# A hand-woven order for VectorE, ScalarE and TensorE up to the last pair, with one factor block, the late turns and the filter tables moved, in an attention and FFT-gate kernel

## The chip, the cores and the metric

The kernel runs on one core of a Trainium2 chip. The metric is the device time of one execution in microseconds (us), here the median of the runs shown. A profiled execution has a time of its own, and a span from its first to its last instruction; both are named where they are used.

## What is computed

Batch 4, 8 heads, 768 positions, head size 64. Some heads (`is_retrieval`) attend to all earlier positions, the others to 4 sink positions and a window of 64. The attention's output, heads side by side, goes into a gate with a circular convolution along the sequence:

```python
scores = np.where(mask, scale * np.matmul(q, k.transpose(0, 1, 3, 2)), -1e9)
a = softmax(scores)                                 # scale = 1/8
x = np.matmul(a, v)                                 # B, H, S, D -> B, S, 512
x1, x2, x3 = split(x @ w_proj)                      # 512 channels each
x2_conv = irfft(rfft(x2) * rfft(filter_fft))        # along the 768 positions
out = (x1 * x2_conv * x3) @ w_out
```

(shortened from the reference). Inputs and output are float32.

## The kernel before

The work is cut into 16 pairs n = 0 to 15: batch b = n // 4 and head pair hp = n % 4. A pair is the attention of two heads; four pairs fill the transposed input xT of one batch's gate.

**A pair.** Loads of q, k and v go out on SP (SyncE) up to three pairs ahead (`emit_loads` L89, `emit_load_v` L97); POOL (GpSimd) casts them to bf16 (`emit_cast` L116, `emit_v` L302). `emit_prep` (L126) turns q and k so that the head dimension lies on the partitions: for n < 6 by TensorE (PE) and a copy on ScalarE (ACT, L140), from 6 on by a transposing DMA on SP (L142). The transposed scores of the causal blocks are computed in six chunks, two in each third (`emit_chunks` L311, matmul L322), each followed by an exp on ACT from PSUM into pT (L329). A mask product on VectorE (DVE) per third (`emit_masking` L331, L336) zeroes what isn't attended. A pair later come the products with v and a column of ones (`emit_values` L339, 42 matmuls, L347), the division (`emit_norm` L354: `rec` L357, `attn` L358, both DVE) and the turn of attn into xT (`emit_turn` L361: six PE transposes L365 and a DVE copy L367 for n < 6 and for the last pair of each batch; a transposing DMA on SP, L369, for the others).

**A gate.** `moe(b, xT)` (L374) is a generator; each `gate_step` (L480) runs it to its next `yield`. Its steps before the change, with the PE work of each:

- x2, three steps: eight 512-column matmuls (L380), a copy on ACT (L384), a sum and a difference on DVE (L385, L386);
- X, three steps: six 512-column matmuls with the Fourier matrix G (`emit_forward` L253, L258), a copy on ACT (L392), products with the filter tables on DVE into P (L395 to L401);
- factors, four blocks of two steps (L404 to L421): eight 384-column matmuls each (L411); the first half is copied by ACT (x1s, L418), the second is multiplied into g by DVE (L420);
- c, four steps: eight 384-column matmuls with the inverse matrix Gi (L427), ACT copy evs (L430), DVE conv and y (L432 to L434);
- out, three steps: eight 512-column matmuls (L439), ACT copy (L448), DMA of the output on SP (L449). The gate of the last batch writes six blocks (L453 to L466).

**Filter tables.** `setup_steps` (L266) folds the filter (DVE, L269, L270) and makes the tables HAB in four more steps: an `emit_forward` each, with copies and edits on ACT and DVE (L275 to L298).

**The order of the work.** The loop over n (from L501) issues scores, masks, values and gate steps in a fixed text order. SP and POOL always run in that order (`manual_schedule`, L105). PE, ACT and DVE run in it only while n < `MANUAL` = 5 (L103, `order.close()` L507); from then on a scheduler arranges their instructions when the program is built, taking the text order as priority. All matmul results share one pool of four PSUM buffers of two banks each (`bank_pair`, L79 to L82), given out in turn.

The Fourier matrix G has tiles 4 to 7, which hold the halves of G2 twice; before the change four DMAs on SP fill them in pair 1 (L517 to L521). The DMA transpose of G to Gi is issued on SP in pair 5 (L572).

Of the kernel before, what the change touches and what calls it, by code (L numbers as in the profile page):

```python
# [10 lines left out]
BF16 = mybir.dt.bfloat16  # L11
# [33 lines left out]
def kernel(  # L45
# [13 lines left out]
    nc = tc.nc  # L59
# [3 lines left out]
    DM = moe_w_proj.shape[0]  # L63
# [20 lines left out]
    state = {}  # L84
# [15 lines left out]
        nc.sync.dma_start(out=vf, in_=v[b, 2 * hp:2 * hp + 2].rearrange("h (t p) d -> p h t d", p=128))  # L100

    BY_PE = 6
    MANUAL = 5  # L103
    engine = mybir.EngineType
    ctx.enter_context(tc.manual_schedule(engines={engine.Pool, engine.SP}))  # L105
    order = ExitStack()
# [135 lines left out]
    def emit_matrix():  # L242

        nc.gpsimd.tensor_scalar(out=G[:, 1, :, 0], in0=par.to_broadcast([128, NM]), scalar1=-2.0, scalar2=1.0,
                                op0=ALU.mult, op1=ALU.add)

    Gi = const.tile([128, 8, NM, 128], BF16, name="Gi")

    def emit_inverse_matrix():
# [121 lines left out]
                in_=st["attn"].rearrange("p t hh d -> p (t hh d)"))  # L371


    def moe(b, xT):  # L374
        x2 = msb.tile([128, 2, NM, DM], BF16, name="x2")
        for m in range(NM):
            ps = bank_pair("x2_ps")
            for half in range(2):
                for cc in range(NC):
                    nc.tensor.matmul(ps[:, half, :], lhsT=xT[:, cc, half * HS + m * 128:half * HS + (m + 1) * 128],  # L380
                                     rhs=wproj[:, cc, DM:2 * DM],
                                     start=(cc == 0), stop=(cc == NC - 1))
            x2s = msb2.tile([128, 2, DM], BF16, name="x2s")
            nc.scalar.copy(out=x2s, in_=ps)  # L384
            nc.vector.tensor_add(x2[:, 0, m, :], x2s[:, 0], x2s[:, 1])  # L385
            nc.vector.tensor_sub(x2[:, 1, m, :], x2s[:, 0], x2s[:, 1])  # L386
            yield
        P = msb.tile([128, 4, 2, DM], BF16, name="P")
        for t in range(3):
            X = msb2.tile([128, 2, DM], BF16, name="X")  # L390
            ps = emit_forward(x2, ((0, 0), (1, 1)), G2) if t == 2 else emit_forward(x2, ((2 * t, t), (2 * t + 1, t)))
            nc.scalar.copy(out=X, in_=ps)  # L392
            yield
            if t == 2:
                nc.vector.tensor_mul(P[:, 2:4], X[:, None].to_broadcast([128, 2, 2, DM]),  # L395
                                     HAB[:, 2].rearrange("p (a r) c -> p a r c", a=2))
                continue
            nc.vector.tensor_mul(P[:, t], X, HA[:, t])  # L398
            m2 = msb2.tile([128, 2, DM], BF16, name="m2")
            nc.vector.tensor_mul(m2, X[:, ::-1, :], HB[:, t])  # L400
            nc.vector.tensor_add(P[:, t], P[:, t], m2)  # L401
        g = msb.tile([128, NC, S], BF16, name="g")
        y = msb.tile([128, NC, S], BF16, name="y")
        for cb in range(NC):  # L404
            ch = slice(cb * 128, (cb + 1) * 128)
            halves = []
            for part in (0, 2):
                ps = bank_pair("x13_ps")
                for s in range(2):
                    for cc in range(NC):  # L410
                        nc.tensor.matmul(ps[:, s, 0:HS],  # L411
                                         lhsT=wproj[:, cc, part * DM + cb * 128:part * DM + (cb + 1) * 128],
                                         rhs=xT[:, cc, s * HS:s * HS + HS],
                                         start=(cc == 0), stop=(cc == NC - 1))
                halves.append(ps[:, :, 0:HS])
                if part == 0:
                    x1s = msb2.tile([128, 2, HS], BF16, name="x1s")
                    nc.scalar.copy(out=x1s, in_=halves[0])  # L418
                    yield
            nc.vector.tensor_mul(g[:, cb, :].rearrange("p (s t) -> p s t", s=2), x1s, halves[1])  # L420
            yield  # L421
        for cb in range(NC):
            ch = slice(cb * 128, (cb + 1) * 128)
            ps = bank_pair("c_ps")
            for r in range(2):
                for n, (tile_no, t, u) in enumerate(((2 * r, r, 0), (2 * r + 1, r, 1), (4 + r, 2, r), (6 + r, 3, r))):
                    nc.tensor.matmul(ps[:, r, 0:HS], lhsT=P[:, t, u, ch], rhs=Gi[:, tile_no],  # L427
                                     start=(n == 0), stop=(n == 3))
            evs = msb2.tile([128, HS], FP32, name="evs")
            nc.scalar.copy(out=evs, in_=ps[:, 0, 0:HS])  # L430
            conv = msb2.tile([128, S], BF16, name="conv")
            nc.vector.tensor_add(conv[:, 0:HS], evs, ps[:, 1, 0:HS])  # L432
            nc.vector.tensor_sub(conv[:, HS:S], evs, ps[:, 1, 0:HS])  # L433
            nc.vector.tensor_mul(y[:, cb, :], conv, g[:, cb, :])  # L434
            yield
        def emit_out(ps, i, cbs):
            for cb in cbs:
                for n in range(ps.shape[1]):
                    nc.tensor.matmul(ps[:, n, :], lhsT=y[:, cb, (i + n) * 128:(i + n + 1) * 128],  # L439
                                     rhs=wout[:, cb, :], start=(cb == 0), stop=(cb == NC - 1))  # L440

        if b < B - 1:
            for i in range(0, NT, 2):
                ps = bank_pair("out_ps")
                for n in range(2):
                    emit_out(ps[:, n:n + 1], i + n, range(NC))
                o_sb = msb2.tile([128, 2, DM], FP32, name="o_sb")
                nc.scalar.copy(out=o_sb, in_=ps)  # L448
                nc.sync.dma_start(  # L449
                    out=out[b, i * 128:(i + 2) * 128, :].rearrange("(n p) c -> p n c", p=128), in_=o_sb)  # L450
                yield
            return
        o_last = pTp.tile([128, NT, DM], FP32, name="o_last", tag="pT")  # L453
        ps = [bank_pair("out_ps")[:, 0:1] for i in range(3)]
        for cbs in ((0, 1), (2,), (3,)):
            for i in range(3):
                emit_out(ps[i], i, cbs)
        for i in range(NT):
            if i >= 3:
                ps.append(bank_pair("out_ps")[:, 0:1])  # L460
                emit_out(ps[i], i, range(NC))
            if i % 2:
                nc.vector.tensor_copy(out=o_last[:, i], in_=ps[i][:, 0])
            else:
                nc.scalar.copy(out=o_last[:, i], in_=ps[i][:, 0])
            nc.sync.dma_start(out=out[b, i * 128:(i + 1) * 128, :], in_=o_last[:, i])  # L466
        yield
# [20 lines left out]
    def emit_weights(n):  # L488
        if n == 0:
            state["filt"] = filt = msb.tile([128, NT, DM], BF16, name="filt", tag="g")  # L490
            nc.gpsimd.dma_start(out=filt, in_=moe_filter_fft.rearrange("(t p) c -> p t c", p=128))
            emit_matrix()
        for part in {2: (1,), 4: (0, 2)}.get(n, ()):
            cols = slice(part * DM, part * DM + DM)
            nc.gpsimd.dma_start(out=wproj[:, :, cols], in_=moe_w_proj.rearrange("(c p) n -> p c n", p=128)[:, :, cols])
        if n == 7:
            nc.gpsimd.dma_start(out=wout, in_=moe_w_out.rearrange("(c p) n -> p c n", p=128))
# [3 lines left out]
    for n, (b, hp) in enumerate(pairs):  # L501
# [12 lines left out]
            emit_v(state[n + 1])  # L514
        if 1 <= n < N - 3:
            emit_loads(n + 3)
        if n == 1:  # L517
            for part in range(2):
                for half in range(2):
                    nc.sync.dma_start(out=G[:, 4 + 2 * part:6 + 2 * part, :, 64 * half:64 * half + 64],  # L520
                                      in_=G2[:, :, :, 64 * part:64 * part + 64])  # L521
        if n < 4:
            if n >= 2:
                emit_turn(state[n - 2])
# [14 lines left out]
                emit_norm(last)  # L539
            emit_chunks(st, 2, 1)  # L540
            emit_masking(st, 1)
            if n == 3:
                gates.append(setup_steps())
                gate_step()
            continue
        if n == 4:
            emit_turn(state[n - 2])
            emit_masking(last, 2)
        elif n + 1 < BY_PE:
            emit_prep(nxt)  # L550
        gate_step()
        emit_values(last)
        emit_norm(last)
        emit_masking(st, 0)
        if n > 4:
            gate_step()
        emit_chunks(st, 1)
        if n == 4:
            gate_step()
        emit_masking(st, 1)  # L560
        emit_turn(last)
        if n == 4:
            emit_prep(nxt)
        if BY_PE <= n + 2 < N:
            emit_prep(state[n + 2])
        gate_step()
        if hp == 0:
            gates.append(moe(b - 1, last["xT"]))
        gate_step()
        emit_chunks(st, 2)  # L570
        emit_masking(st, 2)
        if n == 5:  # L572
            emit_inverse_matrix()
        gate_step()
    last = state[N - 1]
    emit_values(last)
    emit_norm(last)
# [41 lines left out]
```

## Time and profile before

| | us |
|---|---|
| median of 3 runs (lowest to highest) | 225.52 (224.45 to 227.03) |
| profiled execution: its time | 226.71 |
| its span | 225.0 |
| PE busy | 192.8 |
| DVE busy | 160.5 |
| ACT busy | 150.3 |
| POOL busy | 70.6 |
| first scores of pair 4 / 5 / 9 / 13 | 33.06 / 50.28 / 99.27 / 144.67 |
| last attention product (pair 15) | 178.10 |

In a table of stretches each engine has its busy time and, in brackets, its instructions; PEld is PE's loading of weights, PEclk the granted clock of PE as a share of full speed, DMA the mean busy share of the 16 DMA engines. In the list of waits the numbers are: us in total, how often, longest. In a timeline they are: start, duration, then engine, line and operation, and in square brackets the idle time before and what ended it. PE's matmuls overlap, so their pace is read from starts that follow each other.

### The profile page before, as it was taken

Reading aid. Unit: us, or ns where it says so; the run is one execution under the profiler, and the core shown is the slowest. Engines: PE = TensorE matmul, PEld = TensorE weight load, DVE = VectorE, ACT = ScalarE, POOL = GpSimd, SP = SyncE. Lnnn points to the kernel's source line nnn. Section 1 sums busy time; section 2 is a strip of 40 time slices with the busy share of each in tenths; the row PEclk is TensorE's granted clock in tenths of the full one; section 3 lists DMA queues with packets and bytes.
Section 4 is the critical chain, followed back from the end, with each engine's and each line's share of the span. In section 5 each row is a group of like instructions: output and inputs, shape, how many; then the busy total and the mean of one; then the engine's idle time right before and its main releaser. Section 6 shows DMA issues by size and latency. Waiting matters only on the chain.

```text
span 225.0 us, 4244 instructions
## 1 busy us (share of the span) xinstructions
PE 192.8 (86%) x1726; PEld 103.0 (46%) x1726; DVE 160.5 (71%) x251; ACT 150.3 (67%) x183; POOL 70.6 (31%) x99
## 2 busy tenths in 40 slices
PE   1579876779878999799987999899899989999991
PEld 0335554335344645335353654353556644455630
DVE  6979889996896769815697679547876682466681
ACT  7999996657874776187984684779885423662321
POOL 5399447906430643600346062412000000000000
PEclk9999999999999999799999999999999999999999
DMA  5999999999999999648996999298011001500007
GB/s 153 301 297 211 274 188 262 187 222 213 199 184 215 203 183 224 63 186 196 176 221 122 218 180 188 68 309 109 0 38 35 3 1 66 214 3 0 0 3 277
DMA packets 93027, 34.81 MB, mean 155 GB/s; under 512 B 84048, under 2 KB 89936, under 8 KB 93008
## 3 DMA queue, kind: packets, MB, share of 16 engines
q1 hardware_dynamic: 90112, 31.67, 69.5%
q0 software_dynamic: 2896, 2.88, 7.9%
q8 instruction: 13, 0.21, 0.4%
q14 instruction: 6, 0.05, 0.1%
HBM read 24.65 MB, written 6.29 MB: 138 GB/s over the span
## 4 chain that ended last, share of the span: by engine, by line
PE 46%; DVE 29%; ACT 17%; issue 3%; DMA 2%; POOL 0%; SPq 0%; ACTq 0%; DVEq 0%
PE x_ps L411 17%; ACT pT L329 10%; PE out_ps L439 9%; PE x_ps L380 6%; DVE pT L336 5%; PE sc L322 4%; PE att L347 3%; PE c_ps L427 3%; PE X_ps L258 3%; DVE attn L358 3%; DVE y L434 2%; ACT qkT L140 2%; DVE conv L432 2%; DVE P L401 2%; DVE P L398 2%
## 5 line engine op out<-in xcount | busy, mean ns | idle before, releaser
L329 ACT ACTIVATE pT<-sc 128x1024 bf16<-128x1024 f32 x96 | 83.0, 966 | 9.5 <-PE sc L322 9.4
L336 DVE TENSOR_TENSOR pT<-pT,mask 128x1024 bf16<-128x1024 bf16 x48 | 41.8, 873 | 20.9 <-ACT pT L329 20.4
L114 POOL CAST qk_bf<-qk_f 128x768 bf16<-128x768 f32 x31 | 27.1, 878 | 71.8 <-DMA qk_f<-in_q_dram 60.4
L411 PE MATMUL x_ps<-xT,wproj 128*128 128x384 bf16 x256 | 45.3, 326 | 3.4 <-DVE attn L358 1.9
L322 PE MATMUL sc<-qkT 64*128 64x512 bf16 (+3 forms) x256 | 29.9, 326 | 6.5 <-ACT qkT L140 2.5
L411 PEld LDWEIGHTS <-wproj 128*128 128x128 bf16 x256 | 23.8, 98 | 21.1 <-issue 5.6
L347 PE MATMUL att<-v_aug,pT 128*128 128x65 bf16 x352 | 25.3, 197 | 3.1 <-DVE pT L336 2.6
L347 PEld LDWEIGHTS <-pT 128*128 128x128 bf16 x672 | 23.8, 100 | 8.2 <-DVE pT L336 4.1
L420 DVE TENSOR_TENSOR g<-x1s,x_ps 128x768 bf16<-128x768 bf16 x16 | 15.2, 952 | 14.4 <-PE x_ps L411 14.3
L439 PE MATMUL out_ps<-wout,y 128*128 128x512 bf16 x96 | 24.3, 401 | 1.1 <-DVE conv L433 0.6
L380 PE MATMUL x_ps<-wproj,xT 128*128 128x512 bf16 x96 | 22.4, 379 | 1.2 <-DVE HAB L277 1.0
L427 PE MATMUL c_ps<-Gi,P 128*128 128x384 bf16 x128 | 22.8, 326 | 0.0
L418 ACT CAST x1s<-x_ps 128x768 bf16<-128x768 f32 x16 | 12.8, 801 | 14.4 <-PE x_ps L411 14.4
L347 PE MATMUL att<-v_far,pT 128*128 128x65 bf16 x320 | 21.9, 197 | 0.0
L322 PEld LDWEIGHTS <-qkT 64*128 64x128 bf16 x256 | 9.6, 96 | 26.1 <-issue 18.4
L309 POOL TENSOR_TENSOR v_far<-v_aug,vmask 128x520 bf16<-128x520 bf16 x16 | 20.0, 1249 | 1.3
L430 ACT COPY evs<-c_ps 128x384 f32<-128x384 f32 x16 | 7.7, 482 | 15.7 <-PE c_ps L427 10.8
L114 POOL CAST v_aug<-v_f 128x768 bf16<-128x768 f32 x16 | 16.8, 1052 | 3.4 <-DMA v_f<-in_v_dram 3.4
L258 PE MATMUL X_ps<-x,G 128*128 128x512 bf16 x72 | 17.4, 379 | 0.3 <-ACT x2s L384 0.3
L384 ACT CAST x2s<-x_ps 128x1024 bf16<-128x1024 f32 x12 | 12.2, 1018 | 7.5 <-PE x_ps L380 5.3
L448 ACT COPY o_sb<-out_ps 128x1024 f32<-128x1024 f32 x9 | 9.1, 1012 | 10.0 <-PE out_ps L439 9.8
L358 DVE TENSOR_TENSOR attn<-att,rec 128x768 bf16<-128x768 f32 x16 | 15.3, 953 | 0.4
(76 smaller groups left out, 206.6 us busy)
## 6 DMA issues: line engine op xcount, KB each, us to landing
qk_f<-in_q_dram SPq DMA_DIRECT2D x16, 384.0 KB, 6.2
qk_f<-in_k_dram SPq DMA_DIRECT2D x16, 384.0 KB, 6.8
v_f<-in_v_dram SPq DMA_DIRECT2D x16, 384.0 KB, 5.0
out_dram<-o_sb SPq DMA_DIRECT2D x9, 512.0 KB, 3.1
wproj<-in_moe_w_proj_dram POOLq DMA_DIRECT2D x3, 512.0 KB, 7.7
out_dram<-o_last SPq DMA_DIRECT2D x6, 256.0 KB, 2.6
filt<-in_moe_filter_fft_dram POOLq DMA_DIRECT2D x1, 768.0 KB, 9.9
wout<-in_moe_w_out_dram POOLq DMA_DIRECT2D x1, 512.0 KB, 8.7
```

The source lines that it names most:

```text
L114: nc.gpsimd.tensor_copy(out=out, in_=in_)
L258: nc.tensor.matmul(ps[:, u, :], lhsT=matrix[:, t, m, :], rhs=src[:, r, m, :], start=(m == 0), stop=(m == NM - 1))
L309: nc.gpsimd.tensor_mul(v_far, v_aug[:, 0:4], vmask[:, hp, :, :, None].to_broadcast([128, 4, 2, 65]))
L322: nc.tensor.matmul(sc[:, hh, n * 128:(n + cnt) * 128], lhsT=qkT[rows, 1, j * 128:(j + 1) * 128], rhs=qkT[rows, 0, i * 128:(i + cnt) * 128] ...
L329: nc.scalar.activation(out=pT[:, :, c, 0:w], in_=sc[:, :, 0:w], func=AF.Exp, scale=SCALE)
L336: nc.vector.tensor_mul(near, near, kinds)
L347: nc.tensor.matmul(att[:, hh, 65 * i:65 * i + 65], lhsT=st["pT"][:, hh, c, 128 * n:128 * n + 128], rhs=st["v_far" if i >= j + 2 else "v_au ...
L358: nc.vector.tensor_mul(st["attn"].rearrange("p i hh d -> p hh i d"), rows[:, :, :, 0:64], rec[:, :, :, None].to_broadcast([128, 2, NT, 64]))
L380: nc.tensor.matmul(ps[:, half, :], lhsT=xT[:, cc, half * HS + m * 128:half * HS + (m + 1) * 128], rhs=wproj[:, cc, DM:2 * DM], start=(cc = ...
L411: nc.tensor.matmul(ps[:, s, 0:HS], lhsT=wproj[:, cc, part * DM + cb * 128:part * DM + (cb + 1) * 128], rhs=xT[:, cc, s * HS:s * HS + HS], ...
L427: nc.tensor.matmul(ps[:, r, 0:HS], lhsT=P[:, t, u, ch], rhs=Gi[:, tile_no], start=(n == 0), stop=(n == 3))
L439: nc.tensor.matmul(ps[:, n, :], lhsT=y[:, cb, (i + n) * 128:(i + n + 1) * 128], rhs=wout[:, cb, :], start=(cb == 0), stop=(cb == NC - 1))
```

## The change

- `MANUAL` goes from 5 to 15: PE, ACT and DVE run in the order of the text for pairs 0 to 14; the scheduler arranges pair 15 and what follows.
- The doubled tiles of G are written by four POOL copies in pair 3 (`emit_doubles`) in place of four DMAs on SP in pair 1.
- In the gate, the first factor block comes ahead of the X steps, the other three after them.
- The filter tables are made in pairs 4 and 5 (fold, then three steps in pair 4, the fourth in pair 5), the last two woven between the first x2 steps of gate 0 (`between`). Before, the fold was in pair 3 and the four steps in pair 4.
- In pairs 5 to 15 the turn of the pair before comes at the end of the pair, after the q/k transposes and the output DMAs of the middle; only in the first pair of a batch it stays before the start of the new gate. The gate steps are placed anew: five per pair, six in the odd ones.
- x2 and the folded filter have the same memory in both kernels. With the new order the first x2 sums are written there ahead of the last two table steps, which changes those two tables.

```diff
-    MANUAL = 5
+    MANUAL = 15
...
+    def emit_doubles():
+        for part in range(2):
+            for half in range(2):
+                nc.gpsimd.tensor_copy(out=G[:, 4 + 2 * part:6 + 2 * part, :, 64 * half:64 * half + 64],
+                                      in_=G2[:, :, :, 64 * part:64 * part + 64])
...
-    def moe(b, xT):
+    def moe(b, xT, between=()):
...
             yield
+            for step in between:
+                yield
+                break
         g = msb.tile([128, NC, S], BF16, name="g")
         y = msb.tile([128, NC, S], BF16, name="y")
-        for cb in range(NC):
-            ch = slice(cb * 128, (cb + 1) * 128)
+
+        def factors(cb):
             halves = []
...
+        yield from factors(0)
+        P = msb.tile([128, 4, 2, DM], BF16, name="P")
+        for t in range(3):
...
+        for cb in range(1, NC):
+            yield from factors(cb)
...
+        if n == 3:
+            emit_doubles()
...
-        if n == 1:
-            for part in range(2):
-                for half in range(2):
-                    nc.sync.dma_start(out=G[:, 4 + 2 * part:6 + 2 * part, :, 64 * half:64 * half + 64],
-                                      in_=G2[:, :, :, 64 * part:64 * part + 64])
...
-            if n == 3:
-                gates.append(setup_steps())
-                gate_step()
             continue
         if n == 4:
             emit_turn(state[n - 2])
             emit_masking(last, 2)
-        elif n + 1 < BY_PE:
+            setup = setup_steps()
+            next(setup)
+            emit_values(last)
+            emit_norm(last)
+            emit_chunks(st, 1)
+            next(setup)
+            emit_masking(st, 0)
+            emit_turn(last)
+            next(setup)
+            emit_masking(st, 1)
+            emit_prep(nxt)
+            gates.append(moe(b - 1, last["xT"], setup))
+            gate_step()
+            gate_step()
+            emit_prep(state[n + 2])
+            emit_chunks(st, 2)
+            emit_masking(st, 2)
+            gate_step()
+            continue
+        if n + 1 < BY_PE:
             emit_prep(nxt)
         gate_step()
         emit_values(last)
         emit_norm(last)
+        gate_step()
         emit_masking(st, 0)
-        if n > 4:
-            gate_step()
         emit_chunks(st, 1)
-        if n == 4:
-            gate_step()
+        gate_step()
         emit_masking(st, 1)
-        emit_turn(last)
-        if n == 4:
-            emit_prep(nxt)
+        if hp == 0:
+            emit_turn(last)
+            gates.append(moe(b - 1, last["xT"]))
         if BY_PE <= n + 2 < N:
             emit_prep(state[n + 2])
-        gate_step()
-        if hp == 0:
-            gates.append(moe(b - 1, last["xT"]))
         gate_step()
         emit_chunks(st, 2)
         emit_masking(st, 2)
         if n == 5:
             emit_inverse_matrix()
+        if hp != 0:
+            emit_turn(last)
         gate_step()
+        if hp % 2:
+            gate_step()
```

More of the change, by code (lines that the diff above doesn't have):

```diff
@@ L387, in moe @@
             yield
[L388 to L401, printed above, removed]
+            for step in between:
+                yield
+                break
         g = msb.tile([128, NC, S], BF16, name="g")
         y = msb.tile([128, NC, S], BF16, name="y")
-        for cb in range(NC):
-            ch = slice(cb * 128, (cb + 1) * 128)
+        def factors(cb):
             halves = []
@@ L421, in moe @@
             yield
+        yield from factors(0)
+        P = msb.tile([128, 4, 2, DM], BF16, name="P")
+        for t in range(3):
+            X = msb2.tile([128, 2, DM], BF16, name="X")
+            ps = emit_forward(x2, ((0, 0), (1, 1)), G2) if t == 2 else emit_forward(x2, ((2 * t, t), (2 * t + 1, t)))
+            nc.scalar.copy(out=X, in_=ps)
+            yield
+            if t == 2:
+                nc.vector.tensor_mul(P[:, 2:4], X[:, None].to_broadcast([128, 2, 2, DM]),
+                                     HAB[:, 2].rearrange("p (a r) c -> p a r c", a=2))
+                continue
+            nc.vector.tensor_mul(P[:, t], X, HA[:, t])
+            m2 = msb2.tile([128, 2, DM], BF16, name="m2")
+            nc.vector.tensor_mul(m2, X[:, ::-1, :], HB[:, t])
+            nc.vector.tensor_add(P[:, t], P[:, t], m2)
+        for cb in range(1, NC):
+            yield from factors(cb)
         for cb in range(NC):
@@ L548 @@
             emit_masking(last, 2)
-        elif n + 1 < BY_PE:
+            setup = setup_steps()
[16 more added lines that the diff above has]
+            gate_step()
+            continue
+        if n + 1 < BY_PE:
             emit_prep(nxt)
```

## The prediction

> **What bounds the kernel now.** First the share of busy time on the page, then the same by stage.
>
> ```profile
> PE 192.8 (86%) x1726; PEld 103.0 (46%) x1726; DVE 160.5 (71%) x251; ACT 150.3 (67%) x183; POOL 70.6 (31%) x99
> ```
>
> TensorE (PE) has most work, but no engine is full. In the timeline of PE I took the start of each pair's first scores (pair 5 at 50.28, 9 at 99.27, 12 at 132.39, 15 at 166.76) and of the last attention product (178.10), and asked for the busy time between these marks.
>
> ```profile
> core 0: us, PE busy (x) PEld busy (x) DVE busy (x) ACT busy (x) POOL busy (x), PEclk, DMA share, GB/s
> ...
> 74.69:84.25 9.56, 9.56 (x99) 5.48 (x98) 6.66 (x10) 6.91 (x10) 5.77 (x8) 1.00 1.15 201
> 84.25:99.27 15.02, 13.13 (x105) 6.31 (x105) 10.28 (x16) 8.08 (x12) 5.46 (x7) 0.89 0.81 141
> ...
> 110.77:122.84 12.07, 9.77 (x98) 5.36 (x98) 10.37 (x12) 8.09 (x11) 6.99 (x9) 1.00 0.91 165
> 122.84:132.39 9.55, 9.55 (x99) 5.50 (x100) 6.04 (x8) 6.88 (x9) 2.40 (x5) 1.00 1.08 194
> 132.39:144.67 12.28, 11.15 (x106) 5.77 (x106) 10.84 (x19) 7.88 (x12) 5.54 (x7) 1.00 0.99 145
> ...
> sum 127.82, PE 117.74 PEld 61.83 DVE 89.88 ACT 90.91 POOL 39.09; mean PE 10.70 PEld 5.62 DVE 8.17 ACT 8.26 POOL 3.55
> ```
>
> One line is one pair. Pairs 7 and 11 hold the attention of a pair and five gate steps of eight 384-column matmuls: PE never stops, 9.56 and 9.55 us. Where it stops, VectorE (DVE) is at 10 us of 12. Over pairs 5 to 15 PE is idle for 127.8 - 117.7 = 10.1 us. Before that, from 33 to 50 (pair 4 and the filter tables), PE has 11.94 busy of 17.00 and DVE 16.75: DVE is the bound there. After 178.1 there is one gate alone: 41.35 of 47. The waits of PE in 50 to 178 say who ends its pauses:
>
> ```profile
> PE xt_ps L365 <- DVE attn L358: 3.5, 4, 1.8
> PE x_ps L411 <- DVE attn L358: 1.9, 1, 1.9
> PE att L347 <- DVE pT L336: 1.5, 1, 1.5
> ```
>
> The second is what in-order queues do: the attention's PSUM buffer is freed by `attn` (L358), which stands on DVE behind the products P of L398 to L401, and PE needs that buffer. In the timeline of DVE the same product takes 0.69 or 1.3:
>
> ```profile
> 111.06 0.69 DVE L398 TENSOR_TENSOR P<-X,HAB 128x1024 bf16<-128x1024 bf16 x1 [0.47 <-ACT X L392]
> 111.67 1.31 DVE L400 TENSOR_TENSOR m<-X,HAB 128x1024 bf16<-128x1024 bf16 x1
> 112.90 1.30 DVE L398 TENSOR_TENSOR P<-X,HAB 128x1024 bf16<-128x1024 bf16 x1
> ...
> 118.62 0.94 DVE L358 TENSOR_TENSOR attn<-att,rec 128x768 bf16<-128x768 f32 x1
> ```
>
> **What the Trainium skill says.** "SBUF — State Buffer", section Who interferes with whom: a VectorE instruction with two SBUF inputs shares a read interface with GpSimd, and the second to start waits. The doubled durations agree: GpSimd (POOL) is busy 6.99 us in that pair, and from 155 on, with POOL silent, the same products are at 0.69. "Perfetto Trace Analysis", section Identifying the Most-Contended Engine, warns that matmul busy time says little of PE's headroom. It holds here, so I count steps, not shares. [...] The trace has one such stretch, granted clock 0.66 in 92 to 97, right after PE idled for 1.8 us.
>
> **The change part by part.**
>
> *Table copies from SP to POOL.* Four transfers go (6.93 us of SP's issue from 20.09) and four copies of 384 bf16 elements each come on POOL in pair 3. No row shows that copy; a 768-element cast (0.88) and the 520-element product (1.25) bound one at 0.4 to 1.25 us, 1.8 to 5 together; I take 2. POOL waits 4.26 us for q just there (30.7 to 34.98), which hides 2. At 5 the cast at 34.98 starts 0.7 late, and its transposes run only at 42. Without the cover: 2. The loads behind the transfers start up to 7 us sooner, but ACT is full from 10 to 35 whatever arrives. I take 0, from -0.5 to +1.
>
> *Filter tables one pair later.* The fold leaves pair 3; pair 4 gets fold, three filter steps and two x2 steps, the fourth filter step goes to pair 5. Pair 4 is DVE's. On DVE now stand, in this order: xT copy 0.5, mask 0.7, the two folds 2.0 to 2.5, rec and attn 1.2, then, once ACT has put the table, 2.75 of table edits, mask, xT copy, 1.2 + 0.6 of the second table, mask, x2 0.8, 1.2 of the third, mask, x2 0.8: about 14.5, with some 2.5 of waiting for ACT's table: 17, as the 16.75 before. End of pair 4 unchanged; PE did one x2 step more (8 x 0.22 = 1.8) and one filter step less (1.4): 0.4 us less left for later.
>
> *Factor block 0 ahead of the X steps, more steps per pair.* The number of gate steps rises from five to six in the odd pairs. By order, at the last attention the kernel before still has 23 c matmuls (0.163 each by the timeline, 384 columns) and 24 out matmuls (0.213); the changed kernel has 21 out matmuls. So 23 x 0.163 + 3 x 0.213 = 4.4 us of PE work moves ahead of the last attention, and the tail after it, where PE is full anyway, gets 4.4 shorter. The tail's other work is the same.
>
> *Written order up to pair 14, late turns.* Here PE, ACT and DVE take the order of the text. PSUM has four buffers, in rotation. I went through the pairs in the listed order with increments from the timelines: scores 0.43 (thirds 0 to 2: 0.43, 0.48, 0.54), attention 1.28, factor, X and c 1.33, x2 and out 1.75; exp 0.92 (0.72 and 0.5 for short ones), ACT's copies of 1024 0.92, x1s 0.7, evs 0.4; mask 0.6, attn and g 0.95, P and m 0.6 each, conv 0.5 each, y 0.5, xT copy 0.5. Three waits come out.
>
> 1. x2 behind a mask. In pairs 8 and 12 the turn's copy to xT stands on DVE behind mask 1, which waits for exp 3 of the same pair. Pair 12, from its first score: out 1 to 2.15, attention 3.45, out 2 to 5.2, scores 5.65, turn 6.0; the first three matmuls of x2 need only the earlier heads: 6.85. ACT copies out until 6.2, exps to 7.85, mask 8.45, xT 8.95: PE waits 2.2 plus 0.2 before. In pair 8 a third out step stands in between: 0.7. Together 3.1. Behind it on PE: x2, then the scores of third 2.
> 2. out behind the last y. In pair 11 out 0 comes right after c 3. DVE has g, attn, four times conv and y, three masks: 0.95 + 1.15 + 6.0 + 1.8, and from its start at 1.85 ends, with exp waits, at 12.5; PE is at the fourth out matmul at 9.9 and waits 2.6. In pair 8 the scores come between: 1.4. Together 4.0, with the scores of the next pair queued behind.
> 3. attn behind x2 and P. In pair 9 attn ends at 5.85 after the x2 sums, and the second factor half needs its buffer: 0.7. In pair 10, P is held behind mask 2 of pair 9, so X's two buffers free late: 0.6 before the attention, and 0.7 before a factor. Pairs 13 and 14 repeat it (2.0), pairs 5 and 6 have about the same, as x2 stands elsewhere but POOL is busy (2.0), and products doubled by POOL (0.6 more each) add perhaps 0.4 in all: 6.4.
>
> Sum 13.5. In exchange the 10.1 of idle go, since they belong to the scheduler's order. Pairs 5 to 15 then: busy 117.7 + 4.4 - 0.4 = 121.7, plus 13.5 = 135.2, against 127.8: +7.4. Tail -4.4. Net +3.0. The short half-speed stretch (about 2 us in 117.7) I leave in, since there are as many waits that can set it off. Turns on SP now stand behind the loads and q/k transposes of their pair; a turn lands 3.5 us after issue, and its first reader is some 6 us into the next pair: 0, at worst 1 each at pairs 8 and 12.
>
> Span 225.0 + 3.0 = 228.0, profiled execution 226.7 + 3.0. That execution is 1.2 above the median of the runs shown, so the median gives 225.5 + 3.0 = 228.5 us.
>
> **Rivals.** *A, the weave fills PE* (faster). In pairs 7 and 11 five steps at 1.36 between scores ran without a pause; if ACT and DVE keep pace like this and only the two hard waits (x2 in pair 12, out in pair 11: 5 us) remain, the sum is -5.1 + 4.0 - 4.4 = -5.5: 220. It decides once all waits in pairs 5 to 15 are below 8.2, where waits - 10.1 + 4.0 - 4.4 passes -2.25, 1% of 225. For: the mean pair has 8.2 us of DVE and 8.3 of ACT against 10.7 of PE. Against: the load is lumpy, DVE over 10 in three pairs.
>
> *B, the two orders are worth the same.* Waits of 10.5, and no change: 225.5. For: without the half-speed stretch (-2) my own sum nearly gives it.
>
> *C, DVE becomes the bound in the pairs with P and with c.* Contention doubles P, mask and y there: a P phase of six products goes from 3.6 to 7.2, y and masks of pair 11 gain 2; with half of it on the path, 1.8 in each of three P phases and 0.5 in each c phase of pairs 7 and 11, less the 0.4 counted, it is 6 on top: 234.5.
>
> **How the numbers follow.** The mechanism of my sum 0.44 (own range 226 to 232), A 0.24, B 0.20, C 0.12. The predicted time is 228.5. The range, 220.5 to 234, leaves out the far end of A and of C, about 2 in 10. One per cent, about what a measurement of this kernel can tell from none, is 223.3 to 227.8: faster 0.24, same 0.22, slower 0.54.
>
> **What would show it.** PE's waits named `x_ps <- DVE xT` in pairs 8 and 12, `out_ps <- DVE y` at pairs 8 and 11, waits for attn or X in 6, 10 and 14; pairs 9 to 12 near 48 to 50 us against 45.4; the tail after the last attention near 42.5 instead of 46.9; pair 4 still 17. If PE's idle in pairs 5 to 15 is below 8.2, A holds and my reckoning of waits is what failed; if the tail isn't 4 us shorter, the count of moved work is.

## The result, and the profile after

The changed kernel takes 237.76 us (median of 4 executions, 234.28 to 243.13) beside 225.11 of the kernel before on the same chip. Medians, here and in the table below, are of all executions, while a ratio compares only those within 1.5% of each kernel's fastest (here 234.28 and 234.68 us, at a mean granted clock of 0.99, without 240.85 and 243.13, at 0.95). The ratio is 1.0402, 95% interval 1.0289 to 1.0515. A repeat (e10, below) gave 239.42 beside 226.17: 1.0571 (1.0513 to 1.0629). So it is slower, by 4 to 6%, 9 to 13 us; the prediction said slower as the likeliest, by 3.0, and its range ended at 234. The profiled execution took 234.68, span 233.0. What the granted clock does is taken up with e10.

The page of the changed kernel: span, busy shares, granted clock.

```profile
span 233.0 us, 4223 instructions
PE 189.8 (81%) x1710; PEld 101.8 (44%) x1726; DVE 158.4 (68%) x251; ACT 150.4 (65%) x183; POOL 74.1 (32%) x103
PEclk9999999999999999999999999999999999999997
```

PE and DVE have no more work than before (189.8 against 192.8, 158.4 against 160.5), POOL has 3.5 more, and the clock is full up to the last slice. All the loss in this execution is waiting. By stage, each line from one pair's first scores to the next, pairs 4, 5, 8, 11 and 12, and in the last line from the first product of the last attention to the end (columns as in the table of stretches of before):

```profile
34.58:51.57 16.99, 12.38 (x115) 6.31 (x117) 14.07 (x19) 10.45 (x12) 10.33 (x13) 1.00 1.18 177
51.57:67.57 16.00, 11.93 (x105) 6.19 (x107) 10.79 (x17) 9.85 (x12) 7.11 (x10) 1.00 1.20 211
...
89.21:104.60 15.39, 12.34 (x104) 5.65 (x106) 8.09 (x14) 9.04 (x11) 3.57 (x5) 1.00 0.51 141
...
128.35:143.62 15.27, 11.48 (x106) 6.17 (x107) 11.59 (x19) 7.60 (x12) 3.70 (x5) 1.00 0.54 89
143.62:156.50 12.88, 10.59 (x97) 5.00 (x98) 4.07 (x7) 8.57 (x10) 3.32 (x5) 1.00 1.00 226
...
190.69:232.97 42.28, 36.81 (x229) 19.19 (x231) 22.87 (x40) 16.35 (x21) 0.00 (x0) 0.97 0.20 75
```

Duration less PE busy is PE's idle time. Over pairs 5 to 15 it comes to 19.8 us of 139.1, where the kernel before had 10.1 of 127.8; pair 5 alone holds 4.07, pair 11 3.79, pair 8 3.05. No other engine is full in the pairs shown: DVE has 8.09 of 15.39 in pair 8 and 4.07 of 12.88 in pair 12. So it looks like order, not load, which the experiments test. PE's waits over the span (total, times, longest):

```profile
PE x_ps L406 <- DVE attn L364: 4.7, 5, 1.8
PE out_ps L452 <- DVE y L447: 4.5, 5, 1.7
PE x_ps L386 <- DVE xT L373: 4.4, 3, 2.0
PE att L353 <- DVE pT L342: 3.9, 2, 2.9
...
PE c_ps L440 <- DVE conv L446: 1.3, 2, 1.0
```

The first three are the three kinds that the prediction listed. The fourth was not in it. Its largest piece is in pair 5, here with what DVE did before it (timelines of the changed kernel, DVE then PE):

```profile
48.34 0.69 DVE L342 TENSOR_TENSOR pT<-pT,mask 128x1024 bf16<-128x1024 bf16 x1
54.33 0.55 DVE L391 TENSOR_TENSOR x<-x2s 128x512 bf16<-128x512 bf16 x1 [5.30 <-PE X_ps L264]
...
55.24 1.23 DVE L283 TENSOR_SCALAR HAB<-X_ps 64x1024 bf16<-64x1024 f32 x1
56.50 0.69 DVE L342 TENSOR_TENSOR pT<-pT,mask 128x1024 bf16<-128x1024 bf16 x1
```

```profile
52.76 1.46 PE L264 MATMUL X_ps<-fold,G 128*128 128x512 bf16 x6 [0.50 <-ACT x2s L390]
57.25 0.20 PE L353 MATMUL att<-v_aug,pT 128*128 128x65 bf16 x1 [2.88 <-DVE pT L342]
```

The first x2 sum writes into the memory of the folded filter. DVE stands still for 5.30 us until the fourth table step (52.76, on PE behind the first scores of pair 5) has read the fold. Behind the sum stand a table edit and a mask, and the attention of pair 5 waits 2.88 us for that mask. This also corrects the last point of the list in "The change": the sums do not overwrite the fold early, they wait for its last reader, so no table changes. I had listed the overlap and taken it for a matter of values instead of a wait.

### The profile page after: what moved, and what is told of

The parts are those of the page before. It is cut to its first block, busy times and chain, and to the rows that moved or that the text cites. A ratio compares the mean times of both kernels' runs of the same rounds, so it can differ in the third digit from the quotient of the medians.

```text
span 233.0 us, 4223 instructions
## 1 busy us (share of the span) xinstructions
PE 189.8 (81%) x1710; PEld 101.8 (44%) x1726; DVE 158.4 (68%) x251; ACT 150.4 (65%) x183; POOL 74.1 (32%) x103
## 3 DMA queue, kind: packets, MB, share of 16 engines
q0 software_dynamic: 2896, 2.88, 8.0%
## 4 chain that ended last, share of the span: by engine, by line
PE 46%; DVE 26%; ACT 16%; DMA 3%; POOL 3%; issue 3%; SPq 1%; ACTq 0%; DVEq 0%; POOLq 0%
PE x_ps L406 15%; ACT pT L335 10%; PE out_ps L452 8%; PE x_ps L386 7%; PE X_ps L264 6%; DVE pT L342 5%; PE att L353 4%; DMA qk_f<-in_k_dram 3%; PE sc L328 3%; DVE y L447 3%; PE c_ps L440 3%; DVE conv L445 3%; DVE conv L446 2%; DVE attn L364 2%; ACT qkT L140 2%
## 5 line engine op out<-in xcount | busy, mean ns | idle before, releaser
L114 POOL CAST qk_bf<-qk_f 128x768 bf16<-128x768 f32 x31 | 29.7, 967 | 79.2 <-DMA qk_f<-in_q_dram 64.8
L342 DVE TENSOR_TENSOR pT<-pT,mask 128x1024 bf16<-128x1024 bf16 x48 | 38.5, 805 | 14.9 <-ACT pT L335 14.4
L353 PEld LDWEIGHTS <-pT 128*128 128x128 bf16 x672 | 23.5, 99 | 10.9 <-DVE pT L342 4.4
L452 PE MATMUL out_ps<-wout,y 128*128 128x512 bf16 x89 | 22.5, 380 | 5.8 <-DVE y L447 4.5
L440 PE MATMUL c_ps<-Gi,P 128*128 128x384 bf16 x128 | 22.3, 326 | 1.3 <-DVE conv L446 1.3
L328 PEld LDWEIGHTS <-qkT 64*128 64x128 bf16 x256 | 9.4, 97 | 24.1 <-issue 17.2
L391 DVE TENSOR_TENSOR x<-x2s 128x512 bf16<-128x512 bf16 x12 | 6.1, 506 | 19.0 <-ACT x2s L390 13.7
L315 POOL TENSOR_TENSOR v_far<-v_aug,vmask 128x520 bf16<-128x520 bf16 x16 | 18.5, 1156 | 1.3
L423 ACT CAST X<-X_ps 128x1024 bf16<-128x1024 f32 x12 | 12.2, 1017 | 9.6 <-PE X_ps L264 7.3
L264 PE MATMUL X_ps<-x,G 128*128 128x512 bf16 x68 | 16.3, 379 | 0.4 <-DVE g L415 0.2
L440 PEld LDWEIGHTS <-P 128*128 128x128 bf16 x128 | 11.9, 98 | 10.1 <-DVE conv L446 1.6
```

The source lines that it names most:

```text
L114: nc.gpsimd.tensor_copy(out=out, in_=in_)
L264: nc.tensor.matmul(ps[:, u, :], lhsT=matrix[:, t, m, :], rhs=src[:, r, m, :], start=(m == 0), stop=(m == NM - 1))
L315: nc.gpsimd.tensor_mul(v_far, v_aug[:, 0:4], vmask[:, hp, :, :, None].to_broadcast([128, 4, 2, 65]))
L328: nc.tensor.matmul(sc[:, hh, n * 128:(n + cnt) * 128], lhsT=qkT[rows, 1, j * 128:(j + 1) * 128], rhs=qkT[rows, 0, i * 128:(i + cnt) * 128] ...
L342: nc.vector.tensor_mul(near, near, kinds)
L353: nc.tensor.matmul(att[:, hh, 65 * i:65 * i + 65], lhsT=st["pT"][:, hh, c, 128 * n:128 * n + 128], rhs=st["v_far" if i >= j + 2 else "v_au ...
```

## The experiments

Idle means PE's idle in the profiled execution, from stretches as above (of before they end with the first product of the last attention, at 176.22). The ratios are to the kernel before on the same chip.

| kernel | median us | ratio (95%) | idle, pairs 5 to 15 |
|---|---|---|---|
| before | 225.1 to 226.2 | 1 | 10.0 |
| changed | 237.76 | 1.0402 (1.0289 to 1.0515) | 19.8 |
| changed again (e10) | 239.42 | 1.0571 (1.0513 to 1.0629) | 20.7 |
| e1, fold in its own buffer | 236.52 | none | 16.6 |
| e4, turn ahead of the mask | 235.44 | 1.0381 (1.0338 to 1.0424) | 16.7 |
| e6, e1 and e4 together | 229.83 | 1.0153 (1.0084 to 1.0221) | 14.6 |
| e7, attention ahead of the gate step | 228.87 | 1.0131 (1.0072 to 1.0189) | 11.5 |
| e9, out step moved out of pair 11 | 225.31 | 0.9902 (0.9869 to 0.9935) | 8.6 |
| e2, changed with the scheduler | 229.27 | 1.0075 (1.0047 to 1.0104) | 10.9 |
| e8, e7 with the scheduler | 223.14 | 0.9874 (0.9812 to 0.9937) | 9.6 |
| e11, e9 with the scheduler | 222.07 | 0.9844 (0.9802 to 0.9887) | 6.9 |
| e3, before in written order | 233.97 | 1.0338 (1.0318 to 1.0357) | 13.5 |
| e5, before with the POOL copies | 225.02 | 0.9918 (0.9884 to 0.9952) | 7.3 |

**e3: written order alone.** The kernel before, with one number changed.

```diff
-    MANUAL = 5
+    MANUAL = 15
```

> The kernel before with MANUAL at 15 and nothing else: its own placement of steps in written order up to pair 14. Theory (written order costs by itself): 6 to 12 us over the kernel before, with the same named waits on PE (attn, xT copy, y). Rival (written order is harmless, the weave costs): within 2 us of the kernel before.

Measured: 233.97, ratio 1.0338. From PE's waits in it:

```profile
PE out_ps L439 <- DVE y L434: 4.8, 3, 3.0
```

The wait for the last y appears without any of the new weave, as long as in the changed kernel. A wait for an xT copy, which the theory also named, isn't in the list. Written order costs 3.4% on the old text.

**e2: the weave alone.** The changed kernel with `MANUAL = 5`.

> The changed kernel with MANUAL back at 5: the weave, the late turns and the late tables stay, the scheduler arranges PE, ACT and DVE from pair 5 on. Theory (the written order is what costs): the waits for the last y, the xT copy and attn shrink, and the run is 5 to 9 us shorter than the changed kernel, near the kernel before. Rival (the new placement of the steps costs, in whatever order): at most 2 us shorter.

Measured: 229.27, ratio 1.0075 (the medians give 1.017). PE's waits for the last y fall from 4.5 to 0.9 us and those of x2 for xT from 4.4 to 2.3, those of a factor half for attn don't (4.7 to 5.6). With e3 this makes four corners: old text scheduled 1, old text written 1.034, new text scheduled 1.008, new text written 1.040 to 1.057. Most of the loss comes with the written order; the new text as such costs 1 to 2%.

**e1: the fold in other memory.** The changed kernel, one tag changed, so that x2 no longer waits for the fold.

```diff
-        fold = msb.tile([128, 2, NM, DM], BF16, name="fold", tag="x2")
+        fold = msb.tile([128, 2, NM, DM], BF16, name="fold", tag="P")
```

> The changed kernel with the folded filter in the memory of P instead of that of x2 (P is first written in pair 5, after the last table step). In the changed kernel's trace VectorE stood 5.3 us before the first x2 sum, until the fourth table step's matmuls had read the fold, and PE then waited 2.9 us for the mask behind it. Theory (the shared memory holds VectorE): that wait goes, pair 5 shrinks from 16.0 to about 12 to 13 us and the run is 3 to 4 us shorter than the changed kernel. Rival (pairs 4 and 5 are bound by VectorE's table work, whatever memory it uses): less than 1 us.

The timeline of DVE in e1, the same sum as above, and pair 5 in the stretches of e1:

```profile
48.88 0.43 DVE L391 TENSOR_TENSOR x<-x2s 128x512 bf16<-128x512 bf16 x1
```

```profile
52.87:65.96 13.09, 11.97 (x108) 6.15 (x108) 7.99 (x14) 9.84 (x11) 4.25 (x6) 1.00 1.21 209
```

The bracket of 5.30 us is gone, and pair 5 falls from 16.00 to 13.09 us, its idle from 4.07 to 1.12. The wait and its size of 2.9 us are shown. The median, 236.52 (231.75 to 238.88), is blurred by stretches at half clock (e10; the trace of e1 has five), and no ratio is drawn from it.

**e4: the turn ahead of the mask.** In the first pair of a batch, the turn and its copy to xT go ahead of mask 1 on DVE.

```diff
-        emit_masking(st, 1)
         if hp == 0:
             emit_turn(last)
             gates.append(moe(b - 1, last["xT"]))
+        emit_masking(st, 1)
```

> The changed kernel with the turn's copy to xT put ahead of the second mask on VectorE in the first pair of each batch (pairs 8 and 12); PE's order stays. Theory (PE waits 0.6 us in pair 8 and 2.0 in pair 12 for a copy that stands behind a mask that waits for exp): these waits go, 2 to 2.6 us shorter than the changed kernel. Rival (another wait ends last there, ACT's copies or the scores' buffers): less than 0.8 us.

Pair 12 in e4, to be held against 143.62:156.50 above:

```profile
148.80:160.86 12.06, 11.84 (x97) 5.36 (x96) 4.16 (x7) 8.67 (x10) 2.37 (x4) 0.88 0.98 231
```

Idle goes from 2.29 to 0.22, in pair 8 from 3.05 to 2.07: the waits behind the xT copy are gone. But busy went from 10.59 to 11.84 at a clock of 0.88, and pair 12 is only 0.8 us shorter. The time doesn't settle it: the median, 235.44, is 2.3 us below 237.76, as the theory had it, but the ratio, 1.0381, is only 0.2% below 1.0402, and the intervals overlap.

**e6: both.**

> The changed kernel with both earlier edits, the fold in the memory of P and the turn's copy ahead of the second mask in pairs 8 and 12. Theory (the waits are separate and add): PE's idle time in pairs 5 to 15 goes from 19.8 to 13 or 14 us, and at the same granted clock the run is 5 to 6 us shorter than the changed kernel, 228 to 230. Rival (what waits next takes their place): idle above 16 us.

Measured: 229.83 (228.16 to 230.2), idle 14.6. The time lies in the range of the theory, the idle 0.6 above it: in pair 8 the wait behind conv grew from 0.93 to 1.73 us (idle 3.59). Ratio 1.0153 after 1.040 to 1.057: the two edits together are worth 2.5 to 4%, more than the medians of e1 and e4 let see. That fits their traces, which have five drops of the clock each, where that of e6 has two.

**e7: the attention ahead of the gate step,** outside the first pair of a batch: attn no longer stands on DVE behind x2 sums or P.

```diff
-        gate_step()
+        if hp == 0:
+            gate_step()
         emit_values(last)
         emit_norm(last)
+        if hp != 0:
+            gate_step()
```

> As the one before, and in the pairs that are not first in a batch the values and the division come ahead of the first gate step, so that attn stands on VectorE ahead of the x2 sums and the products P. Theory (attn behind those products holds the attention's PSUM buffer in pairs 9, 10, 13 and 14, 0.5 to 2.2 us each): idle in pairs 5 to 15 near 10 or 11 us, 2 to 3.5 us shorter than without it. Rival (the attention then waits for the last mask of the pair before): no gain, and a wait of att for pT in each pair.

Measured: 228.87, 1.0 below e6 and not the 2 to 3.5 of the theory; the intervals of the two ratios overlap, so a gain in time isn't shown. Idle falls in pair 10 from 2.68 to 1.11, in pair 8 from 3.59 to 2.32 and in pair 11 from 3.74 to 2.98, and rises in pair 5 (1.32 to 2.08) and 6 (0.01 to 0.93): 11.5 in all. So a part of the wait moved, though not to where the rival had it: X (1.25 us, pair 5) and a turn (0.88, pair 6) now wait for g, while the attention waits for its mask for 0.58 us in pair 5 and for under 0.2 in any later pair.

**e9: the out step.** On top of e7 the sixth gate step of pair 11 moves to pair 12, and the attention goes ahead of the gate step in every pair.

```diff
-        if hp == 0:
-            gate_step()
         emit_values(last)
         emit_norm(last)
-        if hp != 0:
-            gate_step()
+        gate_step()
         gate_step()
...
-        if hp % 2:
+        if hp % 2 and n != 11:
             gate_step()
```

> On top of e7, the last step of pair 11 (the first out product) moves to pair 12, and in pairs 8 and 12 the values and the division come ahead of it. My theory: the out product stood behind the last y of VectorE; moved behind scores and attention, the 3.0 us of idle TensorE in pair 11 fall below 0.5, pair 8 keeps about 1.5, and the waits named out <- y fall from 4.4 us to about 1. One gate step (1.3 to 1.75 us) goes back behind the last attention. Net -1.5: 226.5 to 228.0 against 228.9 of e7. Rival: VectorE with its y, masks and division is the bound between pairs 11 and 12, and the wait only moves to the first out product in pair 12 or to the first x2 there: idle over pairs 5 to 15 stays near 11.5 and the time is 228.5 to 230.5.

Measured: 225.31 in 22 executions, ratio 0.9902 (the medians give 0.996), below the range of my theory. Part of that is a miscount of mine: no step went back behind the last attention. The tail is 42.26 us as in e7, since one call of `gate_step` in pair 12 had found its gate finished and had done nothing, and the moved steps fill it. Pairs 11 and 12 in the stretches of e7, then of e9, the only wait above 0.2 us in pair 12 of e9, and what DVE did before it:

```profile
125.62:141.32 15.70, 12.72 (x106) 6.42 (x107) 10.76 (x19) 7.60 (x12) 3.51 (x5) 0.92 0.42 70
141.32:152.43 11.11, 10.84 (x97) 5.14 (x98) 4.40 (x7) 8.62 (x10) 1.39 (x2) 0.96 0.97 221
```

```profile
126.48:136.42 9.94, 9.80 (x99) 5.53 (x99) 7.37 (x13) 7.11 (x11) 3.51 (x5) 1.00 1.08 194
136.42:152.16 15.74, 14.09 (x107) 6.55 (x106) 8.43 (x14) 9.06 (x12) 3.79 (x5) 0.89 0.45 129
```

```profile
139.00 0.20 PE L353 MATMUL att<-v_aug,pT 128*128 128x65 bf16 x1 [1.53 <-DVE pT L342]
```

```profile
137.12 1.22 DVE L447 TENSOR_TENSOR y<-conv,g 128x768 bf16<-128x768 bf16 x1
138.26 0.68 DVE L342 TENSOR_TENSOR pT<-pT,mask 128x1024 bf16<-128x1024 bf16 x1
```

Pair 11's idle falls from 2.98 to 0.14. Pair 12 got the step, and its idle rises from 0.27 to 1.65: about half of the wait moved there, as the rival had it, onto the attention, whose mask stands on DVE behind a y. The other half is gone, and pair 8 has 1.66 instead of 2.32. PE, ACT and DVE are in written order up to pair 14 here, and the kernel is as fast as before or 1% faster: what the written order costs depends on the text.

**e8 and e11: the mended texts with the scheduler** (`MANUAL = 5` in e7 and in e9).

> The same text as the one before with MANUAL at 5, so that the scheduler arranges pairs 5 to 15 from it. Theory (the scheduler steps around such waits itself, so mending the text gives it little beyond the fold's memory, about 1 us): 227 to 229 against the 229.3 of the scheduled weave. Rival (the scheduler gains as much as the written order does from the mended text): 223 to 226, below the kernel before.

> The text of e9 with the scheduler from pair 5 on, as e8 was the text of e7. Theory: the scheduler had already filled the wait for the last y in e8, so the moved step changes nothing but the step given back to the tail: 223 to 225 beside 223.1 of e8. Rival: the priority of the text still counts there, and it gains as the written one does: 221 to 222.5.

Measured: 223.14 and 222.07 (six executions, 221.83 to 223.58). Both lie in the range of the rival: I thought that the scheduler makes the text's mends worthless, and it gains from them (1.0075 in e2, 0.9874 in e8), which fits that it takes the text as priority. That it gains from the moved step as much as the written order does isn't shown: from e8 to e11 the ratio goes from 0.9874 to 0.9844, with intervals that overlap, where the written order went from 1.0131 to 0.9902. e11 is the best version found, 1.6% below before.

**e5: the copies alone.** The kernel before, with the four copies on POOL in pair 3 in place of the four DMAs.

> The kernel before with one part of the change: the doubled tiles of G are copied by POOL in pair 3 and not by four DMAs in pair 1. Theory (POOL's 3.0 us of copies lie in its wait for q, the freed DMA issue changes nothing as ACT is full): within 1 us of the kernel before. Rival (the changed kernel's pair 4 starts 1.5 us later because of this part): 1 to 2 us slower.

Measured: 225.02 beside 226.19, ratio 0.9918. It is no loss, and not the cause. Whether the 1.2 us come from the copies or from the new schedule around them is open: pair 4 starts at 33.1 in both, and the difference lies in later pairs.

**e10: the changed kernel again.**

> The changed kernel as it is, for a firmer ratio beside the others of this batch. Theory: 234 to 238, and a profile whose waits are those of the first; the number of 3.4 us stretches at half clock differs. Rival: the first comparison was disturbed and the time is below 233.

Measured: 239.42, above my 234 to 238. The waits are those of the first profile (idle 20.7), but its profiled execution has span 238.4 against 233.0. It has four stretches at half clock where the first profile has none, in pairs 5, 8, 11 and 12, from 55.49, 93.04, 144.24 and 157.89. The first of them:

```profile
55.50:58.91 3.41, 2.80 (x39) 2.31 (x40) 2.95 (x6) 0.00 (x0) 1.72 (x3) 0.50 1.34 229
```

The granted clock is 0.50, each time for 3.41 us. PE was busy for 12.7 us of the four, so some 6.4 us of its work were lost (an estimate, half of that), and pairs 5 to 15 are 7.6 longer than in the first profile (146.7 against 139.1), of which 0.8 is idle. The starts of the four lie 11, 15 and 4 times 3.413 us apart. The 3.41 us just before each of them:

```profile
52.08:55.49 3.41, 0.12 (x4) 0.00 (x0) 3.28 (x4) 1.31 (x2) 1.63 (x2) 1.00 1.29 230
89.62:93.04 3.42, 1.10 (x7) 0.21 (x3) 3.35 (x7) 1.98 (x3) 2.02 (x2) 1.00 0.44 96
140.82:144.24 3.42, 0.87 (x5) 0.14 (x3) 3.26 (x7) 0.48 (x1) 0.00 (x0) 1.00 0.00 0
154.48:157.89 3.41, 1.02 (x5) 0.41 (x5) 1.64 (x2) 0.66 (x1) 1.77 (x4) 1.00 1.16 335
```

PE was busy for a third of each or less. They hold the waits for the mask behind the fold (3.92 us), for y in pairs 8 and 11, and for xT in pair 12. In the first profile the clock drops once, at 230.33, after the last matmul. The windows of 3.41 us that lie whole multiples before that drop, at the same four waits:

```profile
52.83:56.25 3.42, 1.54 (x11) 0.71 (x10) 1.89 (x3) 2.73 (x3) 1.69 (x2) 1.00 1.31 224
90.38:93.79 3.41, 1.61 (x6) 0.62 (x8) 2.45 (x5) 1.30 (x2) 1.42 (x2) 1.00 0.11 18
138.17:141.58 3.41, 1.50 (x8) 0.61 (x7) 3.38 (x7) 0.48 (x1) 0.00 (x0) 1.00 0.00 0
151.82:155.23 3.41, 2.19 (x14) 0.93 (x15) 1.16 (x2) 0.90 (x1) 2.13 (x4) 1.00 1.14 339
```

Here most of these waits fall across the borders, PE is busy for 0.44 to 0.64 of each window, and no drop follows. Counted so, the thirteen traces have 760 such windows at full clock. Each of the 32 with PE busy for less than 0.44 of the window was followed by half clock, none of the 687 above 0.63, and 10 of the 41 in between. So whether a wait is followed by a drop goes with how it lies to these windows, and such a wait costs its own length and up to 1.7 us more (half of 3.41). This is a count over traces; no run moved a wait against the windows on purpose.

## Why the prediction was wrong

The direction was right, and so was the mechanism that it gave most chance: the waits of written order outweigh the idle that they replace. The size failed, by one term of the sum: the waits of pairs 5 to 15, put at 13.5 us, measured 19.8. The account against the profiled execution, span 228.0 forecast, 233.0 measured:

| step of the prediction | forecast | measured | difference |
|---|---|---|---|
| copies, start of pair 4 | 33.1 | 34.6 (33.1 in e10) | +1.5 |
| filter tables, pair 4 | 17.2 | 17.0 | -0.2 |
| pairs 5 to 15, PE busy | 121.7 | 119.3 | -2.4 |
| pairs 5 to 15, waits | 13.5 | 19.8 | +6.3 |
| tail | 42.5 | 42.3 | -0.2 |

Sum +5.0. The median stands 4.3 further off: I put it 1.2 below the profiled execution, as before, and it is 3.1 above it.

Pair 4 took its 17 us in part by luck. The forecast counted the first x2 sums in it, at 0.8 us a step and with no wait; they ran in pair 5, behind the fold, and that wait is in the fourth line.

**Copies: right.** The four take 3.02 us on POOL (estimate 2, bounds 1.8 to 5), under its wait for q:

```profile
31.10 3.02 POOL L250 COPY G<-G 128x384 bf16<-128x384 bf16 x4
```

The late start of pair 4 in the first profile isn't theirs, since e10 has the same text and starts at 33.06.

**Moved work: right.** Tail 42.28 in this kernel and 42.25 to 42.29 in every other with the new weave. PE busy is 2.4 lower than forecast: 1.7 of it is the half-speed stretch that I had left in (3.41 us in the kernel before, none in this profile); the rest is open, and 16 of the 1726 matmuls are missing from this trace. Of the signs that I named, pairs 9 to 12 took 51.9 us against 48 to 50, and pair 6 shows no wait for attn or X.

**The sum of the waits: the step that failed.** By place, measured from the brackets in PE's timeline:

| wait | forecast | measured |
|---|---|---|
| x2 behind the xT copy, pairs 8 and 12 | 0.7 + 2.4 | 0.63 + 2.24 |
| out behind the last y, pairs 8 and 11 | 1.4 + 2.6 | 1.43 + 2.76 |
| attn and X, pair 9 | 0.7 | 0.40 |
| attn and X, pair 10 | 1.3 | 2.22 |
| attn and X, pairs 13 and 14 | 2.0 | 2.88 |
| pairs 5 and 6 | 2.0 | 3.87 |
| c or out behind conv, pairs 8 and 11 | 0 | 1.96 |
| contention; the rest (pairs 7, 15, short gaps) | 0.4 | 1.4 |

The two kinds that were walked through instruction by instruction came out within 0.25 us each. Their lines, PE's timeline of the changed kernel, two for out in pair 11 and one for x2 in pair 12:

```profile
140.31 0.39 PE L452 MATMUL out_ps<-wout,y 128*128 128x512 bf16 x1 [1.03 <-DVE y L447]
142.44 1.25 PE L452 MATMUL out_ps<-wout,y 128*128 128x512 bf16 x5 [1.73 <-DVE y L447]
...
153.04 1.25 PE L386 MATMUL x_ps<-wproj,xT 128*128 128x512 bf16 x5 [2.02 <-DVE xT L373]
```

Three other kinds of term failed.

First, terms filled in by likeness, 2.75 of the 6.3 us. "Pairs 5 and 6 have about the same" was a guess, and the pair with the shared memory stood in it: 2.88 of its 3.87 is the mask behind the x2 sum behind the fold, which e1 took away. "Pairs 13 and 14 repeat it" left out that POOL works there: the two sums that stand ahead of attn take 0.98 and 1.27 us, where others take 0.41.

```profile
158.10 0.41 DVE L392 TENSOR_TENSOR x<-x2s 128x512 bf16<-128x512 bf16 x1
160.45 0.98 DVE L391 TENSOR_TENSOR x<-x2s 128x512 bf16<-128x512 bf16 x1 [1.93 <-ACT x2s L390]
161.35 1.27 DVE L392 TENSOR_TENSOR x<-x2s 128x512 bf16<-128x512 bf16 x1
```

The division stands behind them, and PE's factor half waits 1.81 us for it. POOL has a cast from 160.32 and a product from 161.23. This agrees with what the prediction took from the Trainium skill, "SBUF — State Buffer", section Who interferes with whom.

Second, the same lengthening in pairs that I had walked. In pair 10 two products ahead of attn take 1.19 and 1.84 us, where the same ones take 0.69 and 1.22 in pair 14, and the waits came to 2.22 instead of 1.3:

```profile
119.66 1.19 DVE L432 TENSOR_TENSOR P<-P,m 128x1024 bf16<-128x1024 bf16 x1
120.77 1.84 DVE L426 TENSOR_TENSOR P<-X,HAB 128x2048 bf16<-128x2048 bf16 x1
```

It also hit a mask in pair 11 (1.53 at 135.07), and c then waited 1.03 for conv. I priced all of it at 0.4. No run took POOL's work out of these pairs, so its share is read from the traces and not shown by an experiment.

Third, a wait that the walk of pairs 8 and 11 had at nothing: PE behind conv, 0.93 us in pair 8 and the 1.03 in pair 11.

**The half-speed stretch: failed.** I left one in "since there are as many waits that can set it off". Within pairs 5 to 15 the changed kernel has none in one profile and four in the other, by how its waits lie to the windows of 3.41 us (e10). That fits the 4.3 us by which the median is off; it is shown by the trace of e10, not for each execution.

**Turns on SP: right.** No wait of PE names a turned xT from SP; only the copy by DVE is waited for.

**The rivals.** A (waits below 8.2) and B (waits of 10.5) fell for the changed kernel; e9, with idle of 8.6 and 0.9902, lies near the 8.2 from which A was to begin. C gave 234.5, the nearest number, for a reason that is only partly there: contention doubles products, but DVE is not the bound in the pairs that lost most, and moving steps (e9) took the waits away with DVE's work unchanged.

## What to carry to other kernels

Before writing an order by hand, walk every engine's queue through each place where its text differs, the odd places at the seams above all: two kinds of wait that were walked came out within a few tenths, while the terms filled in by likeness, and the products that POOL lengthens, held most of the error. The Trainium skill, "PSUM — Partial Sum Buffer", section Engine vs sequencer instructions, says that the queues of ScalarE, VectorE and GpSimd are strictly first in, first out, and the mask held 5.30 us behind the x2 sum agrees; so ask of each instruction on them what it waits for and what stands behind it, buffers that are shared under another name included, and put what PE needs next (a turn, a division) ahead of what it needs later (a mask, a sum). Four such moves were worth about 14 us here (239.42 to 225.31) and brought the same weave to the kernel before or 1% below it; with the scheduler the mended text was better still (0.9844 beside 0.9902, the intervals just overlap).

## What was not expected of the hardware

TensorE ran at half clock in stretches of 3.41 us, in some traces two in a row, after a window of the same length in which it had been busy for 0.62 of the time or less; each costs up to 1.7 us. The Trainium skill, "TensorE: Matmul & The Clock Gate", section HAM oscillation — how this bites in real kernels, puts the bound at idle gaps over about 3.4 us. Here shorter pauses were followed by a drop (1.63 us in pair 8 and 1.74 in pair 11 of e10, each with another pause in the same window), so in these traces the drops go with the idle time summed over a window and not with one gap. The kernel before has one such stretch in pairs 5 to 15, the changed kernel none in one profile and four in the other. That filling the pauses alone would remove them was not tried apart from removing the waits.
